# Moving the ranks and scatters of a routed block earlier in a fused attention and mixture-of-experts kernel

## The chip, the cores and the metric

The kernel runs on one core of a Trainium2 chip, in one launch. The metric is the device time of an execution in microseconds (us). "Before" is the kernel without the change; its times and one profiled execution are all that the prediction had.

## What is computed

```python
# r, k, v: (4, 8, 768, 48); w, u: (8, 48)
for t in range(S):
    cur = einsum('bhd,bhe->bhde', u * k[t], v[t])
    y[t] = einsum('bhd,bhde->bhe', r[t], state + cur)
    state = w * state + einsum('bhd,bhe->bhde', k[t], v[t])
x = y as (3072 tokens, 384)
x = relu(x @ w_in) ** 2 @ w_out                      # hidden size 2048
logits = x @ w_gate + log1p(exp(x @ w_noise)) * noise # 8 experts
top 2 experts of each token, softmax weights over the two
out = sum over the two: weight * relu(x @ w1[e]) @ w2[e]   # hidden size 1024
```

## The kernel before

The sequence is worked in chunks of 128 tokens (number q, 24 of them) and blocks of 512 (number j, 0 to 5). A block is four chunks.

Three stages overlap. A fixed list (`HEAD`) makes the first chunks' attention. Then a loop over the six blocks (L1063) runs the dense layer: for each f of 16, `mm1(j, f)` (L532, nine products of 128x128 by 128x512), its squared relu `gsplit` (L542, ScalarE and VectorE), and, two f later (`LAG = 2`), `mm2` (L558, mostly nine products again). After every such group stands one of 32 numbered places, 0 to 31, of the block: place 2f follows `mm1(j, f)`, place 2f+1 the `mm2` after it. All other work of the loop is put into these places by a hand-written table; the fraction of a number orders the work within a place. What is put there in block j: attention of the chunks of block j+1 (`CHUNKS`), the routing of block j-1 (`ROUTE`), and, in block 1, the clearing of the buffer `sent`. The third stage, after the loop, runs the experts and is not touched.

Each engine works through its own instructions in the order in which they were put. The places therefore order VectorE, GpSimd (POOL in the rows) and the DMA queue of SyncE as well as TensorE, but an engine runs ahead of the places as far as its inputs are ready.

Attention of a chunk in blocks 1 to 4, in the order of its steps: `pre` (L386; two GpSimd multiplies into `rk`), `p_tr r` and `p_tr k` (L426; a VectorE transpose, then a GpSimd multiply into `rT` or `kT`; the k one also issues the loads of the next chunk), `pre2` (L410; a VectorE sum `dg`, then GpSimd `am` and `vx`), `p_kv` (L494; 32 short products, VectorE adds into `Z`, two GpSimd multiplies of `Z`, L511), `p_a` (L454; 16 short products that read `kT` and `rT`, L459, then VectorE copies into `am`), `p_y` in two parts (L468; 24 short products with `Z`, then 32 with `am`, all L477), and `p_x` (L515). In block 1 the chunks are 8 to 11.

Routing of a block: four times `r_row` (logits), `r_soft1` to `r_sel` (small VectorE work), `r_w1` (one ScalarE exponential), `r_rank` (L701; three small products and seven VectorE operations: the place `si` of every token in `sent`), `r_w2` (L685; eight VectorE operations: weights into `row`), and eight times `r_send` (L729): a small GpSimd memset and one indirect DMA from GpSimd (L732) that scatters 128 rows of 393 floats to `sent`.

`zeros(e)` (L366) clears the places of expert e in `sent`, 1,375.5 KB each, from SyncE; the eight of them are put into block 1, places 3.6 to 13.6. Every scatter writes somewhere in `sent`, so the first one waits for all eight clearings; only the scatters among themselves are declared independent (L735). `zero_out` (L375) clears the output in five parts of 960 KB from SyncE, and its first call fills a zero tile that takes over the memory of the one `zeros` reads.

Of the kernel before, what the change touches and what calls it, by code (L numbers as in the profile page):

```python
# [64 lines left out]
         (3.13, 4.58, 7.33, 8.47),  # L65
         (3.22, 3.43, 3.45, 4.38))

ROUTE = ((4.54, 6.46, 8.84, 9.01, 9.55, 9.63, 10.54, 11.58, 13.491, 14.56, 14.65, 21.81, 20.25,
# [5 lines left out]
CLEAR = {3: (8.7, 14.7, 26.7), 4: (8.7, 14.7)}  # L74
FETCH_00 = 16.7
TURN_00 = ((21.8, 22.8), (23.8, 24.8), (25.8, 26.8))

# [15 lines left out]
def body(ctx, tc, r, k, v, w, u, w_in, w_out, w_gate, w_noise, noise, w1, w2, out):  # L93
# [969 lines left out]
    for j in range(NB):  # L1063
        slots = [[] for _ in range(2 * NF)]

        def put(n, fn, *args):
            k = int(n)
            slots[k].append((n - k, len(slots[k]), lambda: fn(*args)))
# [15 lines left out]
        if j == 1:  # L1084
            for i, n in enumerate(SPLIT_AT):
                put(n, split_out, i)
            for e in range(E):
                put(e * 3 // 2 + 3.6, zeros, e)
        for i, n in enumerate(CLEAR.get(j, ())):
            put(n, zero_out, i + sum(len(c) for k, c in CLEAR.items() if k < j), sum(map(len, CLEAR.values())))  # L1090
        if j:
            plan = [(r_row, i) for i in range(TPB)] + [(fn,) for fn in (r_soft1, r_soft2, r_soft3, r_top1, r_top2, r_sel, r_w1, r_rank, r_w2)]
            plan += [(r_send, *divmod(i, 2)) for i in range(2 * TPB)]
            for n, (fn, *args) in zip(ROUTE[0 if j == 1 else 1 if j < NB - 1 else 2], plan):
                put(n, fn, j - 1, *args)
# [171 lines left out]
```

## Time and profile before

| what | us |
|---|---|
| median of 3 runs | 951.79 (951.4 to 951.82) |
| the profiled execution, its own time | 954.92 |
| span of the profiled execution, first to last instruction | 953.1 |
| TensorE (PE) busy in it | 938.8 |
| GpSimd (POOL) busy in it | 349.2 |

The profiled execution took 3.1 us more than the median, and 1.8 us of its time lie around its span. Block 1 begins 118.5 us after the span's start, block 2 at 204.2, block 3 at 287.5, block 4 at 371.6, block 5 at 455.2.

### The profile page before, as it was taken

How to read it: one execution, taken by the hardware profiler on the slowest of the kernel's cores; microseconds unless marked ns; L12 is line 12 of the kernel's file. 1: busy time of each engine (PE TensorE's matmuls, PEld its weight loads, DVE VectorE, ACT ScalarE, POOL GpSimd, SP SyncE). 2: the span in 40 equal slices, each digit the busy share in tenths (PEclk: the TensorE clock that was granted, in tenths of full speed). 3: DMA queues.
4: the chain of work that ended last, by engine and by line, in shares of the span. 5: the costliest groups of instructions: out<-in, count | busy, mean ns of one | idle time of the engine just before them, and what ended most of it. 6: DMA issues, size and time to landing. Idle time of an engine off the chain costs nothing.

```text
span 953.1 us, 17746 instructions
## 1 busy us (share of the span) xinstructions
PE 938.8 (98%) x6845; PEld 805.3 (84%) x6845; DVE 540.4 (57%) x982; ACT 432.9 (45%) x792; POOL 349.2 (37%) x406
## 2 busy tenths in 40 slices
PE   8899999999999999999999999999999999999997
PEld 7677787778778878877888899999999898989987
DVE  8999756636845663684254564554545555356420
ACT  5666655334434444443555542443444444444321
POOL 6665353544573354455030344122121221212112
PEclk9999999999999999999999999999999999999999
DMA  7655379932432464442024367466545565545212
GB/s 179 165 163 165 96 191 302 244 108 64 94 104 56 111 153 122 111 99 86 1 100 93 108 134 188 104 135 135 130 97 115 120 121 109 114 92 109 36 21 37
DMA packets 193233, 112.32 MB, mean 118 GB/s; under 512 B 131777, under 2 KB 185698, under 8 KB 193122
## 3 DMA queue, kind: packets, MB, share of 16 engines
q1 hardware_dynamic: 181698, 91.03, 37.7%
q0 software_dynamic: 10624, 19.74, 11.3%
q8 instruction: 75, 1.23, 0.5%
q14 instruction: 36, 0.29, 0.1%
q10 hardware_dynamic: 800, 0.02, 0.0%
HBM read 74.64 MB, written 36.12 MB: 116 GB/s over the span
## 4 chain that ended last, share of the span: by engine, by line
PE 90%; DVE 5%; issue 1%; POOL 1%; ACT 1%; DMA 1%; POOLq 0%; DVEq 0%; ACTq 0%
PE ph L540 20%; PE xo L571 19%; PE ph L861 19%; PE y L918 14%; PE y L949 4%; PE att L477 3%; PE ph L949 2%; PE att L459 2%; PE att L604 2%; PE y L861 2%; PE xo L565 1%; PE att L962 1%; PE att L503 1%; DVE am L463 1%; DVE t L279 1%
## 5 line engine op out<-in xcount | busy, mean ns | idle before, releaser
L929 POOL DMA_INDIRECT out<-yt,id x56 | 87.1, 1556 | 298.1 <-ACT yt L927 257.4
L555 DVE TENSOR_TENSOR gl<-g,gh 128x512 fp32r<-128x512 f32 x90 | 77.2, 857 | 127.3 <-ACT gh L553 124.2
L904 DVE SCALAR_TENSOR_TENSOR hl<-ph,hh 128x512 fp32r<-128x512 f32 (+1 forms) x112 | 66.9, 599 | 113.1 <-ACT hh L903 109.2
L545 ACT ACTIVATE rt<-ph 128x512 f32<-128x512 f32 x96 | 57.1, 595 | 150.9 <-PE ph L540 146.4
L540 PE MATMUL ph<-x1h,wih 128*128 128x512 f32 x288 | 119.4, 414 | 0.0
L861 PE MATMUL ph<-xh,w0h 128*128 128x512 f32 (+3 forms) x336 | 118.1, 352 | 0.0
L861 PE MATMUL ph<-xl,w0h 128*128 128x512 f32 (+3 forms) x336 | 116.3, 346 | 0.2 <-DVE xl L830 0.2
L861 PE MATMUL ph<-xh,w0l 128*128 128x512 f32 (+3 forms) x336 | 116.1, 346 | 0.0
L540 PE MATMUL ph<-x1h,wil 128*128 128x512 f32 x288 | 112.4, 390 | 0.0
L540 PE MATMUL ph<-x1l,wih 128*128 128x512 f32 x288 | 112.3, 391 | 0.0
L571 PE MATMUL xo<-gh,wol 128*128 128x512 f32 x270 | 105.9, 392 | 0.0
L903 ACT ACTIVATE hh<-ph 128x512 fp32r<-128x512 f32 (+1 forms) x112 | 58.6, 524 | 88.9 <-PE ph L861 84.0
L918 PE MATMUL y<-w1h,hh 128*128 128x384 f32 x256 | 85.7, 335 | 0.0
L918 PE MATMUL y<-w1l,hh 128*128 128x384 f32 x256 | 85.6, 335 | 0.0
L918 PE MATMUL y<-w1h,hl 128*128 128x384 f32 x256 | 85.6, 334 | 0.0
L732 POOL DMA_INDIRECT sent<-row,si x48 | 50.3, 1049 | 61.4 <-DVE gl L555 45.0
L571 PE MATMUL xo<-gh,woh 128*128 128x512 f32 x180 | 71.6, 398 | 0.0
L571 PE MATMUL xo<-gl,woh 128*128 128x512 f32 x180 | 70.1, 390 | 0.0
L861 PEld LDWEIGHTS ph<-xl,w0h 128*128 128x128 f32 x336 | 63.3, 188 | 8.0 <-DVE xl L830 1.3
L861 PEld LDWEIGHTS ph<-xh,w0l 128*128 128x128 f32 x336 | 63.2, 188 | 7.7
L861 PEld LDWEIGHTS ph<-xh,w0h 128*128 128x128 f32 x336 | 63.3, 188 | 6.9 <-ACT xh L829 0.3
L540 PEld LDWEIGHTS ph<-x1h,wih 128*128 128x128 f32 x288 | 54.0, 188 | 16.4 <-issue 3.7
(234 smaller groups left out, 2145.5 us busy)
## 6 DMA issues: line engine op xcount, KB each, us to landing
ws<-in_moe_w SPq DMA_DIRECT2D x128, 96.0 KB
ws<-in_moe_w SPq DMA_DIRECT2D x32, 384.0 KB
sent<-zero SPq DMA_DIRECT2D x8, 1375.5 KB
G<-sent SPq DMA_DIRECT2D x36, 192.0 KB
stg<-in_moe_w_in SPq DMA_DIRECT2D x8, 768.0 KB
stg<-in_moe_w_out SPq DMA_DIRECT2D x8, 768.0 KB
out<-zero SPq DMA_DIRECT2D x5, 960.0 KB
lv<-in_v SPq DMA_DIRECT2D x24, 192.0 KB
```

The source lines that it names most:

```text
L477: nc.tensor.matmul(pb[32 * n:32 * n + 32, d, :], x, y, skip_group_check=True, **kw)
L540: nc.tensor.matmul(ph, wt[qi][:, d, sl], xt[j][:, d, :], start=(n == 0), stop=(n == 3 * KD - 1))
L545: nc.scalar.activation(rt, ph, AF.Relu)
L555: nc.vector.tensor_tensor(gl, g, gh.bitcast(F32), op=OP.subtract)
L571: nc.tensor.matmul(XO[j][:, d, :], wt[qi][:, fo, sl], gt, start=(f == 0 and n == 0), stop=(f == NF - 1 and n == 2))
L732: st = nc.gpsimd.indirect_dma_start(out=sent, in_=s["row"][:, i, :], in_offset=None, out_offset=bass.IndirectOffsetOnAxis(ap=s["si"][:, i, ...
L861: nc.tensor.matmul(ph[:, c], wt[:, d, sl], xt[:, d, c], start=(m == 0), stop=(m == 3 * KD - 1))
L903: nc.scalar.activation(hh[:, :n], ph, AF.Relu)
L904: nc.vector.scalar_tensor_tensor(hl[:, :n], ph, 0.0, hh[:, :n].bitcast(F32), op0=OP.max, op1=OP.subtract)
L918: nc.tensor.matmul(py, ht[:, sl], wt[:, fo, :], start=(m == 0), stop=(m == 3 * NF2 - 1))
L929: st = nc.gpsimd.indirect_dma_start(out=out, in_=yt, in_offset=None, compute_op=OP.add, out_offset=bass.IndirectOffsetOnAxis(ap=IDX[e, un] ...
L949: nc.tensor.matmul(py[d][:, c], wt[:, fo, sl], ht[:, c], start=(m == 0), stop=(m == 3 * NF2 - 1))
```

## The change

It moves routing steps between places, and one of the five parts of the output clearing from block 3 to block 2. Nothing is added or removed.

```diff
-ROUTE = ((4.54, 6.46, 8.84, 9.01, 9.55, 9.63, 10.54, 11.58, 13.491, 14.56, 14.65, 21.81, 20.25,
-          25.32, 26.97, 30.88, 25.84, 25.99, 21.93, 31.39, 31.66),
-         (4.94, 7.82, 9.35, 9.61, 10.1, 13.34, 13.45, 13.47, 13.721, 14.31, 20.46, 19.12, 21.54,
-          24.75, 22.9, 28.29, 28.16, 23.33, 24.72, 21.55, 28.65),
+ROUTE = ((4.54, 6.46, 8.84, 9.01, 9.55, 9.63, 10.54, 11.58, 13.491, 14.56, 14.65, 16.9, 16.5,
+          18.4, 19.3, 20.2, 23.2, 24.0, 24.8, 25.6, 27.8),
+         (4.94, 7.82, 9.35, 9.61, 10.1, 13.34, 13.45, 13.47, 13.721, 14.31, 14.7, 16.1, 16.5,
+          17.6, 18.3, 19.6, 20.3, 21.8, 22.5, 27.4, 28.1),
          (4.22, 4.4, 5.4, 5.47, 5.64, 6.68, 7.8, 7.81, 8.7, 9.5, 9.6, 11.9, 11.6,
           12.6, 13.2, 13.8, 14.4, 15, 15.6, 16.2, 16.6))
-CLEAR = {3: (8.7, 14.7, 26.7), 4: (8.7, 14.7)}
+CLEAR = {2: (16.7,), 3: (8.7, 14.7), 4: (8.7, 14.7)}
```

The first row of `ROUTE` is for block 1, the second for blocks 2 to 4, the third for block 5. The last eleven numbers of a row are `r_w1`, `r_rank`, `r_w2` and the eight scatters. In block 1 the rank goes from place 21 to 16 and the scatters from places 21 to 31 to places 18 to 27; in blocks 2 to 4 the rank goes from 19 to 16, `r_w2` from 21 to 16, and the scatters from 21 to 28 to 17 to 22, with two at 27 and 28. The attention steps stay where they were: in block 1 `p_y` 0 of chunk 9 at 18.64, `pre2` of chunk 10 at 20.4, `p_kv` of chunk 9 at 21.33, `p_tr k` of chunk 10 at 22.28, `pre`, `p_tr r` of chunk 11 and `p_kv` of chunk 10 at 22.4, 22.61 and 22.63, `p_tr k` of chunk 11 at 24.26, `pre2` of chunk 11 at 25.89, `p_a` of chunk 11 at 28.47.

## Rows read from the trace of the kernel before

**Rows 1.** The page: busy us of each engine.
```profile
PE 938.8 (98%) x6845; PEld 805.3 (84%) x6845; DVE 540.4 (57%) x982; ACT 432.9 (45%) x792; POOL 349.2 (37%) x406
```

**Rows 2.** Waits of PE from 118 to 530 us: total, times, longest.
```profile
PE att L503 <- issue: 0.8, 2, 0.4
PE att L477 <- issue: 0.7, 2, 0.4
```

**Rows 3.** Chain that ended last, block 1: start, us, what.
```profile
162.00 2.04 PE xo L571 x9
...
185.75 0.79 PE att L477 x24
...
192.18 1.09 PE att L459 x16
193.27 2.27 PE xo L571 x9
...
198.81 1.01 PE att L477 x20
...
202.13 2.27 PE xo L571 x9
```

**Rows 4.** Timeline of PE, blocks 2 and 3: start, us, what.
```profile
265.62 0.55 PE L503 MATMUL att<-lv,kp 128*32 128x48 f32 x32
...
354.07 0.35 PE L503 MATMUL att<-lv,kp 128*32 128x48 f32 x15
...
355.84 0.50 PE L540 MATMUL ph<-x1h,wih 128*128 128x512 f32 x1
```

**Rows 5.** Timeline of SP: the last three clearings of `sent`.
```profile
158.85 6.72 SPq L372 DMA_DIRECT2D sent<-zero  x3
```

**Rows 6.** Stretches: us, busy of PE, PEld, DVE, ACT, POOL, clock, DMA share, GB/s.
```profile
174.00:176.00 2.00, 2.00 (x13) 1.37 (x16) 1.87 (x10) 0.00 (x0) 0.37 (x1) 1.00 1.08 297
176.00:178.00 2.00, 2.00 (x68) 1.84 (x68) 1.86 (x6) 1.75 (x3) 2.00 (x3) 1.00 1.15 188
```

**Rows 7.** The scatter's line, all of it: semaphore events of its queue.
```profile
L732 POOLq EVENT_SEMAPHORE  x11: 17/17/916, 177.8 to 560.8; - x11
```

**Rows 8.** Timeline of POOL, block 1: start, us, what [idle before].
```profile
175.63 1.90 POOL L421 TENSOR_TENSOR am<-ident,dg 128x1024 f32<-128x1024 f32 x1 [8.07 <-DVE dg L414]
...
177.72 1.08 POOL L511 TENSOR_TENSOR Z<-Z,wmid 48x192 f32<-48x192 f32 x2
...
179.85 1.20 POOL L732 DMA_INDIRECT sent<-row,si  x1 [0.91 <-POOL gap L731]
...
182.37 1.02 POOL L395 TENSOR_TENSOR rk<-lr,lk 128x384 f32<-128x384 f32 x1
...
184.44 1.74 POOL L432 TENSOR_TENSOR rT<-rT,pow 112x512 f32<-112x512 f32 x1
186.15 1.08 POOL L511 TENSOR_TENSOR Z<-Z,wmid 48x192 f32<-48x192 f32 x2
187.31 1.29 POOL L432 TENSOR_TENSOR kT<-kT,pow 112x512 f32<-112x512 f32 x1
188.54 0.09 POOL L731 MEMSET gap<- 1x1 f32 x1
...
191.31 1.90 POOL L421 TENSOR_TENSOR am<-ident,dg 128x1024 f32<-128x1024 f32 x1
```

**Rows 9.** Waits of POOL from 118 to 530 us: total, times, longest.
```profile
POOL Z L511 <- DMA sent<-row,si: 5.3, 3, 4.1
```

**Rows 10.** Timeline of DVE, blocks 1 and 2: start, us, what.
```profile
162.23 0.16 DVE L673 TENSOR_TENSOR tot<-pre,sel 128x8 bf16<-128x8 bf16 x1
...
257.79 0.18 DVE L711 TENSOR_TENSOR rk<-att,base 128x32 f32<-128x32 f32 x1
...
259.68 0.17 DVE L724 CAST si<-slot 128x8 int32<-128x8 f32 x1 [0.21 <-DVE slot L722]
```

**Rows 11.** The last stretch of the execution: columns of rows 6.
```profile
948.00:953.00 5.00, 0.00 (x0) 0.00 (x0) 0.00 (x0) 0.00 (x0) 0.89 (x1) 0.54 0.36 44
```

## Prediction

> **What bounds the kernel now.** I read the page's busy times first: TensorE works 938.8 of 953.1 us [rows 1], so time can be gained or lost only where TensorE waits, and a transfer or another engine matters only by making it wait. Next the waits of TensorE, in the loop alone: two pairs, 1.5 us in all, both named "issue", so no engine or transfer is seen to release them [rows 2]. Then the places. At the end of block 1 stand 56 short products in one row, and they take 202.13 - 198.81 = 3.32 us [rows 3]. Undisturbed, 24 take 0.79 [rows 3], so 56 some 1.84: 1.5 us are lost. In block 3 a `p_kv` of 32 products takes 355.84 - 354.07 = 1.77 us where one in block 2 takes 0.55 [rows 4]: 1.2 lost. So all that the touched loop can give back is 2.7 us, 0.28% of the median. Both gaps lie where scatters run beside long rows of short products.
>
> Everything else in the loop is a cost if it makes TensorE wait. So I followed, for each moved step, what stands behind it on its engine and when TensorE wants that.
>
> **Block 1: the scatters meet the clearing.** The first scatter waits for all eight clearings of `sent`. The last three were issued from 158.85 to 165.6 us [rows 5], and the DMA engines, with a share of 1.08, still moved 297 GB/s from 174 to 176 and fell to 188 only in the next 2 us [rows 6]. The scatter's queue passed its first semaphore event at 177.8 [rows 7], just before the scatter could have run anyway (179.85, [rows 8]). I take 177.8 as the landing; nothing ahead of it changes, so the change can't bring it forward.
>
> Now the order on GpSimd. Before, the first scatter (place 21.93) comes behind `am` and `vx` of chunk 10 and `Z` of chunk 9. After, three scatters (18.4, 19.3, 20.2) stand ahead of these. GpSimd reaches them in the 8.07 us that it now sits idle before 175.63 [rows 8], and blocks until 177.8. Queued behind the blocked scatter is everything GpSimd owes to attention. Step by step, with starts and distances of [rows 8]:
>
> - The first scatter starts up to 0.91 us after the step before it (the idle time at 179.85); I take 0.7 from the release, so 178.5, and 1.20 for itself. Two more take 191.31 - 188.54 = 2.77 with their memsets: 182.5.
> - `am` and `vx` 177.72 - 175.63 = 2.09: 184.6. `Z` of chunk 9 187.31 - 186.15 = 1.16: 185.7.
> - A multiply of `Z` behind scatters was seen to wait for their landing, three times, 4.1 us at most [rows 9]. Here 0 to 0.5, the third scatter having been issued 3 us earlier.
> - `kT` of chunk 10 188.54 - 187.31 = 1.23, the two `rk` 184.44 - 182.37 = 2.07, `rT` of chunk 11 1.3 (as `kT`) to 1.71, `Z` of chunk 10 1.16: together 5.8 to 6.2, so 191.5 to 192.4.
> - The scatters at 23.2 and 24.0, both ahead of `kT` of chunk 11 (24.26): 2.77. Then `kT` 1.23: it is ready at 195.5 to 196.4, where before it was ready at 188.5.
>
> TensorE wants that `kT` for `p_a` of chunk 11 at 192.18 [rows 3]. It waits 3.3 to 4.2 us. I take 3.4, near the lower figure, because some of the rows ran slowed beside other work, and 2.8 as the lower end. Earlier waits are inside this number, since its end is fixed by the clearing: `p_y` 0 of chunk 10 wants `Z` of chunk 9 at 185.75 [rows 3], which is now ready at 185.7 to 186.2, and the rank's products come at place 16, just before the group at 162.00 [rows 3], when `tot` is ready only at 162.23 + 0.16 = 162.39 [rows 10]: at most 0.5 each. What is late next is `am` of chunk 11, two scatters and itself behind `kT` (2.77 + about 1.9), at about 200.4, and VectorE's copies follow; TensorE, itself 3.4 late, wants them after 203 (198.81 + 3.4 + 0.79, [rows 3]) and finds them ready.
>
> **Blocks 2 to 4.** The rank costs VectorE 259.85 - 257.79 = 2.1 us [rows 10], and `r_w2`'s eight small operations I take at about 1.5 by the same row's pace (0.18 each). 3.6 us more at place 16 delays the `gl` that follow. They are wanted two f later, which is four large groups of 2.04 to 2.27 us [rows 3], over 8 us, so TensorE sees nothing. No clearing of `sent` is outstanding. On GpSimd six scatters of 1.4 us (half of 2.77, [rows 8]) fit into places 17 to 22, which hold few other GpSimd steps; nothing of chunk work behind them is wanted before place 24. Price 0; were the cover gone, 1.4 us a scatter.
>
> **The gaps.** In block 3 no scatter stands in places 23 to 26 any more. If its gap needs scatters beside the short products, 1.2 us come back. In block 1 the late start pushes the last scatters (24.8, 25.6, 27.8) to 196 to 202, so with the products 3.4 us later they meet the same row of 56 again; I expect 0 to 1.5 back. Whether the gaps exist in a run without the profiler is open too: the profiled execution took 3.1 us more than the median, enough to hold all of them. The bounds are 0 and 2.7; I take 0.6, half of block 3's.
>
> [...]
>
> **The output clearing.** A part of 960 KB occupies the DMA engines 3 to 5 us (at the 297 to 188 GB/s of [rows 6]). In block 2, place 16.7, it is queued on SyncE behind the loads of place 15.7 that VectorE wants at 17.96, and the next loads are wanted after place 22: hidden. If it did delay a wanted load, VectorE would be up to 5 us late, inside the 8 us of cover just named. In block 3 its absence shortens the 4.1 us that a `Z` multiply waited [rows 9], which TensorE never saw [rows 2]. 0.
>
> **Sum.** 3.4 - 0.6 = +2.8 us. Against the profiled execution's own 954.92 that is 957.7; against the median, 951.8 + 2.8 = 954.6.
>
> **Rivals.** I call a change of more than 0.2% (1.9 us) one that a measurement of this kernel can tell.
>
> - *Forecast, 44%:* GpSimd blocks behind the clearing and `p_a` of chunk 11 waits 2.8 to 4.1; 0 to 1.2 of the gaps return. 953.4 to 955.9.
> - *Wait and both gaps cured, 18%:* 3.4 - 2.7 = +0.7, 952.5. For it: places 24 and 26 are free of scatters by design; against: block 1's late scatters.
> - *Faster, 17%:* the blocked scatters cost TensorE nothing, because the clearing lands before about 174.4, 3.4 us sooner, which is where the sum for `kT` meets 192.18; both gaps go. 951.8 - 2.7 = 949.1, or 949.6 with the rank's wait. Against: the DMA rate to 176 [rows 6].
> - *Nothing moves, 13%:* the wait is hidden and the gaps are the recorder's: 951.8.
> - *The clock falls, 8%:* TensorE's clock was granted at 1.00 (2.4 GHz) through all its short waits and fell to 0.54 in the last stretch, where it had nothing to do [rows 11]. If a wait of 3.4 us dropped it to 1.2 GHz, each large group of nine would take 2.04 us more [rows 3] until it rose; one or two: 957 to 959. [...]
>
> The likeliest gives 954.6, by itself 953.4 to 955.9. The range goes down to the faster case and leaves out the clock: 949.1 to 956.2. Slower 44 + 8 = 52%; within 0.2% 18 + 13 = 31%; faster 17%.
>
> **What would show it.** In the profile after: GpSimd idle from about 168 to 178 before a scatter in block 1; `p_a` of chunk 11 (L459) waiting for GpSimd about 3 us near 192 to 196; block 2 beginning 2 to 3.5 us later than 204.2; no gap in `p_kv` of block 3. The prediction is wrong if the first scatter of block 1 runs well before 177, or if `kT` of chunk 11 is ready by 192.

## The result, and the profile after

The changed kernel took 959.01 us (median of 4 runs, 958.37 to 961.0) against 951.79 for the kernel before (4 runs, 951.4 to 951.82): a ratio of 1.008, 95% interval 1.0064 to 1.0096. That is 7.2 us slower where +2.8 (954.6) was forecast, and outside the predicted range of 949.1 to 956.2. The profiled execution took 961.0 with a span of 959.2.

The blocks, each from its first `mm1` product (L540) to the next block's, in the two profiles:

| block | before, us | after, us |
|---|---|---|
| 1 | 85.76 (with the 1.5 us gap) | 92.73 |
| 2 | 83.23 | 83.88 |
| 3 | 84.09 (with the 1.2 us gap) | 82.77 |
| 4 | 83.65 | 83.81 |

So the loss is in block 1; block 2's 0.65 holds a stop of 0.4 us in a row of short products at 281.9. The waits of TensorE in the loop after (total, times, longest); none of them stood in [rows 2]:

```profile
PE att L459 <- POOL gap L731: 3.8, 1, 3.8
PE att L477 <- POOL Z L511: 0.2, 1, 0.2
PE att L707 <- DVE pre L671: 0.2, 1, 0.2
```

The first is `p_a` of chunk 11, the place that the prediction named. (The releaser is printed as the memset behind `kT` on GpSimd, because `kT` ended just before it.) GpSimd's timeline of block 1 after, to be laid beside [rows 8]:

```profile
167.73 0.09 POOL L731 MEMSET gap<- 1x1 f32 x1
179.05 1.56 POOL L732 DMA_INDIRECT sent<-row,si  x1 [11.23 <-ACT gh L553]
...
182.21 0.97 POOL L732 DMA_INDIRECT sent<-row,si  x1 [0.22 <-issue]
183.21 1.91 POOL L421 TENSOR_TENSOR am<-ident,dg 128x1024 f32<-128x1024 f32 x1
...
186.67 0.51 POOL L511 TENSOR_TENSOR Z<-Z,wmid 48x192 f32<-48x192 f32 x1 [0.87 <-DMA sent<-row,si]
187.26 1.28 POOL L432 TENSOR_TENSOR kT<-kT,pow 112x512 f32<-112x512 f32 x1
188.49 1.48 POOL L395 TENSOR_TENSOR rk<-lr,lk 128x384 f32<-128x384 f32 x1
...
191.00 1.27 POOL L432 TENSOR_TENSOR rT<-rT,pow 112x512 f32<-112x512 f32 x1
192.24 1.53 POOL L511 TENSOR_TENSOR Z<-Z,wmid 48x192 f32<-48x192 f32 x2
...
196.43 1.50 POOL L432 TENSOR_TENSOR kT<-kT,pow 112x512 f32<-112x512 f32 x1
```

GpSimd stands for 11.23 us before the first scatter, all its attention work behind it. The releaser printed there, a ScalarE step, writes nothing that a scatter reads. The scatter's queue stood at one of its semaphores for 8.98 us (8984 ns, the longest event of its line), from 169.1 to 178.1, when the indices `si` had been ready since 169.8:

```profile
L732 POOLq EVENT_SEMAPHORE  x13: 17/17/8984, 166.7 to 567.5; - x13
```

What landed at 178.0 was the last clearing; its semaphore is the one that ended that event. The traffic runs down there (columns as in [rows 6]):

```profile
174.00:176.00 2.00, 2.00 (x39) 1.59 (x39) 1.77 (x4) 0.04 (x1) 0.00 (x0) 1.00 1.06 300
176.00:178.00 2.00, 2.00 (x61) 1.57 (x63) 0.00 (x0) 0.94 (x2) 0.00 (x0) 1.00 1.16 209
196.00:198.00 2.00, 0.01 (x2) 0.02 (x2) 0.69 (x1) 0.09 (x1) 1.90 (x3) 0.93 0.61 214
198.00:200.00 2.00, 2.00 (x17) 1.78 (x17) 0.00 (x0) 0.00 (x0) 1.67 (x3) 0.50 0.21 74
...
206.00:208.00 2.00, 2.00 (x24) 1.43 (x26) 0.55 (x1) 0.25 (x1) 0.00 (x0) 1.00 0.49 98
```

The column after POOL is TensorE's granted clock. From 196 to 198 TensorE did nothing; then, from 197.73 on and for 6.83 us, the clock was 0.50 while TensorE was fully busy, and 1.00 again by 206. The chain that ended last after, to be laid beside [rows 3]:

```profile
196.43 1.50 POOL kT L432
...
197.99 2.08 PE att L459 x16
200.06 4.14 PE xo L571 x9
204.20 1.19 PE att L477 x32
205.39 2.27 PE ph L540 x9
207.65 1.67 PE att L477 x56
```

`p_a` takes 2.08 in place of 1.09, the nine products of `mm2` 4.14 in place of 2.27. And the row of 56 takes 1.67, not 3.32: its gap is gone. So is block 3's (start, us, what):

```profile
356.31 0.48 PE att L503 x32
```

Two amounts make up the 8.6 us of block 1 above an undisturbed block of 84.11 (the profile of the second experiment):

- **Late.** Counted from the block's start, `p_a` of chunk 11 begins at 197.99 - 118.70 = 79.3; before it was 192.18 - 118.48 = 73.7 [rows 3]. That is 5.6 us: the 3.8 of the wait, 0.65 around the rank's three products at place 16, and 1.1 in `p_y` 0 and `p_a` of chunk 10, which took longer behind the late `Z` and `kT`.
- **Half clock.** From the start of `p_a` to the next `mm1` it is 205.39 - 197.99 = 7.4 us, where before it was (198.81 - 2.27) - 192.18 = 4.4. That is 3.0.

### The profile page after: what moved, and what is told of

Its sections match the earlier page's. It is cut to its first block, busy times and chain, and to the rows that moved or that the text cites. A ratio compares the mean times of both kernels' runs of the same rounds, so it can differ in the third digit from the quotient of the medians.

```text
span 959.2 us, 17751 instructions
## 1 busy us (share of the span) xinstructions
PE 942.2 (98%) x6845; PEld 807.7 (84%) x6845; DVE 541.5 (56%) x982; ACT 433.4 (45%) x792; POOL 349.7 (36%) x406
## 3 DMA queue, kind: packets, MB, share of 16 engines
q8 instruction: 75, 1.23, 0.5%
## 4 chain that ended last, share of the span: by engine, by line
PE 83%; DVE 7%; POOL 3%; DMA 3%; issue 2%; ACT 1%; SPq 1%; POOLq 0%; DVEq 0%; ACTq 0%
PE ph L861 19%; PE ph L540 16%; PE xo L571 16%; PE y L918 13%; PE y L949 5%; PE att L477 2%; PE ph L949 2%; PE att L604 2%; PE y L861 2%; PE att L459 2%; DMA sent<-row,si 1%; PE xo L565 1%; DVE am L463 1%; PE att L962 1%; DVE gl L555 1%
## 5 line engine op out<-in xcount | busy, mean ns | idle before, releaser
L555 DVE TENSOR_TENSOR gl<-g,gh 128x512 fp32r<-128x512 f32 x90 | 83.2, 924 | 139.2 <-ACT gh L553 139.1
L540 PE MATMUL ph<-x1h,wih 128*128 128x512 f32 x288 | 119.2, 414 | 0.0
L540 PE MATMUL ph<-x1h,wil 128*128 128x512 f32 x288 | 112.5, 391 | 0.0
L540 PE MATMUL ph<-x1l,wih 128*128 128x512 f32 x288 | 112.3, 391 | 0.0
L918 PE MATMUL y<-w1h,hh 128*128 128x384 f32 x256 | 85.7, 335 | 0.0
L540 PEld LDWEIGHTS ph<-x1h,wih 128*128 128x128 f32 x288 | 54.0, 188 | 16.4 <-issue 3.5
```

The lines of the kernel that those rows point to most:

```text
L540: nc.tensor.matmul(ph, wt[qi][:, d, sl], xt[j][:, d, :], start=(n == 0), stop=(n == 3 * KD - 1))
L555: nc.vector.tensor_tensor(gl, g, gh.bitcast(F32), op=OP.subtract)
L918: nc.tensor.matmul(py, ht[:, sl], wt[:, fo, :], start=(m == 0), stop=(m == 3 * NF2 - 1))
```

## The experiments

The theory: block 1's scatters alone make the loss, first through `kT` of chunk 11, then through the clock that falls in the wait. The main rival: the wait is small change, and the loss is spread over the new row of blocks 2 to 4 and the moved clearing; later, that the half clock costs nothing that the wait had not cost already.

Three chips were used. On the first (four kernels) the kernel before took 951.78 us (19 runs), on the second 955.08 (23 runs), on the third 954.92 (17 runs), so each result is set against its own. The record names no chip for the result above and for the first profile of the kernel before; by its times the result belongs with the first chip.

**Block 1's row alone.** The new first row of `ROUTE`; all else as before.

```diff
-ROUTE = ((4.54, ..., 14.65, 21.81, 20.25, 25.32, 26.97, 30.88, 25.84, 25.99, 21.93, 31.39, 31.66),
+ROUTE = ((4.54, ..., 14.65, 16.9, 16.5, 18.4, 19.3, 20.2, 23.2, 24.0, 24.8, 25.6, 27.8),
```

> Only block 1's row of ROUTE is the changed one; blocks 2 to 4 and the output clearing are as before. Clearing theory (three scatters ahead of GpSimd's attention steps wait for the clearings of sent, kT of chunk 11 is late, TensorE waits 3.8 us and its clock then halves): the whole loss and no return from block 3, so 6 to 9 us over before, 958 to 961, with a TensorE wait of 3.5 to 4.2 us at the p_a of chunk 11 and a stretch at half clock behind it. Spread theory (the loss comes from ranks and weights that now crowd VectorE in blocks 1 to 4, or from the moved output clearing): at most a third of the loss, 952 to 954.5.

Measured: 959.97 (959.81 to 960.07), ratio 1.0087 [1.0072, 1.0103], +8.2. The same wait of 3.8 at L459, the clock at 0.5 for 6.83 us behind it, block 1 92.13. Block 1's row alone makes a loss as large as the whole one. In this execution block 3, scheduled as before, took 82.77: its gap did not occur.

**Blocks 2 to 4 and the clearing alone.** The second row of `ROUTE` and `CLEAR` of the change; block 1 as before.

> The other part alone: blocks 2 to 4 and the output clearing as changed, block 1 as before. Clearing theory: no loss; if the gap of 1.2 us in block 3's p_kv is there without the profiler too and goes, 950.3 to 951.2, and if the gap is only the profiler's, 951.5 to 952.2. Spread theory: 4 to 6 us over before, 956 to 958.

Measured: 953.39 (951.77 to 953.91, 11 runs), ratio 1.0015 [1.0006, 1.0024], +1.6. The profiled execution took 951.77, and no wait of TensorE stands in its loop. The median lies above both ranges of the first expectation and well below that of the second: the loss is not spread, but a remainder of 0.6 to 2.3 us, by the interval, is there that was not expected, and the last two runs below take it up. The two parts alone make 8.2 + 1.6 = 9.8 us and the change 7.2, so they do not simply add up. Block 1, scheduled as before, took 84.11: no gap there either.

**Two scatters behind `kT`.** The change, with the scatters of places 23.2 and 24.0 put behind `kT` of chunk 11 (24.26).

```diff
-          18.4, 19.3, 20.2, 23.2, 24.0, 24.8, 25.6, 27.8),
+          18.4, 19.3, 20.2, 24.3, 24.4, 24.8, 25.6, 27.8),
```

> The changed kernel, but the two scatters of places 23.2 and 24.0 in block 1 stand at 24.3 and 24.4, just behind kT of chunk 11. Clearing theory: kT of chunk 11 is ready about 2.7 us sooner, TensorE waits about 1 us at the p_a of chunk 11, and, the wait being short, the clock stays at 2.4 GHz: 951 to 953.5. If the clock fell for another reason than the length of this wait: 955 to 957. Spread theory: unchanged, 958 to 960.

Measured: 956.19 (956.04 to 957.43), ratio 1.0047 [1.0031, 1.0062], +4.4. The waits of TensorE in the loop:

```profile
PE att L477 <- DVE am L463: 1.1, 1, 1.1
PE att L459 <- POOL gap L731: 1.0, 1, 1.0
...
```

Taking 2.6 us from the chain ahead of `kT` takes 2.8 from the wait at L459. The clock stays at 1.00 in block 1. But `am` of chunk 11 is now behind the moved scatters, and TensorE waits 1.1 us for it: block 1 takes 87.72, and the time is 2.7 above the expected range. (The profiled execution, 957.43, is 1.2 over the median. Its clock fell for 6.83 us in block 0, whose schedule is the same in every kernel here, and block 0 took 86.97 where it takes 85.7 without a fall.)

**All eight scatters behind `kT`.** As before it, but the eight at 24.3, 24.4, 24.8, 25.6, 26.0, 26.1, 26.2 and 27.8.

> The changed kernel, but all eight scatters of block 1 stand behind kT of chunk 11 (24.3, 24.4, 24.8, 25.6, 26.0, 26.1, 26.2, 27.8); the rank stays early. Clearing theory: no wait of TensorE at the p_a of chunk 11, no fall of the clock, 949.5 to 952, the spread being what the gaps of blocks 1 and 3 give back. Spread theory: still 956 or more, since the ranks stay early.

Measured: 953.68 (953.21 to 955.61, 9 runs), ratio 1.0022 [1.0012, 1.0032], +1.9. One wait in the loop is left:

```profile
PE att L707 <- DVE pre L671: 0.2, 1, 0.2
```

`am` of chunk 10 starts 56.6 us into the block (57.2 before the change, [rows 8]), and block 1 takes 84.76, 0.65 above the undisturbed 84.11; the rank's products at place 16 are what is left of the change there. The time is 1.7 above the expected range; what block 1 does not explain of the +1.9, some 1.2, is near the remainder of blocks 2 to 4 and the clearing alone (+1.6). With the scatters behind `kT` the wait at L459 is gone, so the order on GpSimd made it.

**Work in the wait.** The change, with 30 dummy transposes just ahead of `p_a` of chunk 11.

```diff
     def p_a(q, *tag):
-        a = A[q]
+        a = A[q]; [nc.tensor.transpose(pw[:, :P], ident, ident) for pw in ([bank()] if q == 11 else []) for _ in range(30)]
```

> The changed kernel with 30 dummy transposes of 128x128 on TensorE just ahead of p_a of chunk 11 (work that is not in the computation and goes into a bank of its own). They fill the 3.8 us in which TensorE waited for kT of chunk 11. Clock theory (3.4 us of the loss are the 6.83 us at a granted clock of 0.5 that follow the idle wait): GpSimd's chain is as late as in the changed kernel, so p_a still starts near 198, but the clock is then 1.00, the groups after it take 2.27 again and block 1 is 3 to 3.5 shorter: 955.3 to 956.5. Rival (the half clock has another cause than the idle wait, or the groups would be that long anyway): 958.4 to 960, with the clock at 0.5 in the profile all the same.

Measured on the second chip: 958.87 (956.71 to 959.69), ratio 1.0033 [1.0022, 1.0044] to a kernel before of 955.08, +3.8, above the range that was put in microseconds of the first chip. The clock did not fall in block 1, which took 88.81 (it did fall in block 0, for 3.41 us). As the chip was another one, the run was made again beside the changed kernel itself, on the third chip:

> The changed kernel once more, on the same chip as the kernel with 30 filler transposes and the kernel before. In the executions with the two 1.5-us gaps the kernel before took 955.1, in those without 951.8, and the changed kernel has no long row beside its scatters in either place. If the gaps are what tells the two apart, the changed kernel is 958.4 to 960 whichever of the two the kernel before shows (its 3.8 of wait and 3.4 of half clock stay), so +7.2 against a kernel before of 951.8, and +3.5 to +5 against one of 955.1.

> The changed kernel with 30 dummy transposes ahead of p_a of chunk 11, as in the run filler, now beside the changed kernel itself. Clock theory: 2.5 to 4 us faster than the changed kernel of the same runs, with no half clock behind p_a of chunk 11. Rival (the half clock costs nothing that the wait had not cost already): within 1 us of it.

Measured: the changed kernel 960.64 (959.12 to 961.27), ratio 1.0059 [1.0045, 1.0072]; with the dummy work 957.55 (956.69 to 959.07), ratio 1.0032 [1.002, 1.0043]: 3.1 us faster for work added. The first, +5.7, came out 0.6 above what was expected of it. The stretch of `p_a` in the changed kernel's profile:

```profile
196.00:198.00 2.00, 0.16 (x2) 0.17 (x4) 0.66 (x1) 0.00 (x0) 1.78 (x4) 1.00 0.55 200
198.00:200.00 2.00, 2.00 (x17) 1.78 (x18) 0.00 (x0) 0.00 (x0) 1.78 (x3) 0.51 0.26 92
```

and with the dummy work:

```profile
196.00:198.00 2.00, 1.49 (x19) 1.19 (x18) 0.00 (x0) 0.00 (x0) 1.76 (x4) 1.00 0.11 35
198.00:200.00 2.00, 2.00 (x9) 1.40 (x8) 0.00 (x0) 0.00 (x0) 1.84 (x2) 1.00 0.45 171
```

TensorE's timeline with the dummy work (L455) shows that the wait is covered, not removed; 0.51 us of it stay idle:

```profile
192.75 3.44 PE L455 MATMUL att<-ident 128*128 128x128 f32 x30
196.69 1.16 PE L459 MATMUL att<-rT,kT 48*128 48x128 f32 x16 [0.51 <-POOL gap L731]
```

From the start of `p_a` to the next `mm1` it is 201.06 - 196.69 = 4.4 us here, as in the kernel before, and 203.84 - 197.84 = 6.0 in the changed kernel's profile of this chip, where the half clock lasted 3.41 us, not 6.83. So the profiles put 1.6 of the 3.1 down to the clock; `p_a` also began 0.6 sooner in the block, and block 2 was 0.4 shorter. The rival is out, and the clock cost 1.6 us in the one profile and 3.0 in the other.

**Half as much of it.** 12 transposes in place of 30.

> As filler, but with 12 transposes, some 1.6 us by the pace of the warm-up transposes (0.13 each), so that about 2.2 of the 3.8 us stay idle. If an idle stretch of 2.2 us is enough for the clock to fall, 958.4 to 960 and 0.5 in the profile for some 6.8 us; if it is not, 955.3 to 956.5 as with filler. The trace of the kernel before had no idle stretch of that length, so I hold both possible and lean to no fall.

Measured on the second chip: 960.51 (959.73 to 963.94), ratio 1.0061 [1.0045, 1.0077], +5.4 and 1.6 more than with 30. I had leaned to no fall; the clock fell, for 3.41 us from 198.34 on, 1.6 us after an idle stretch of 2.47 had ended:

```profile
192.77 1.47 PE L455 MATMUL att<-ident 128*128 128x128 f32 x12
196.71 1.16 PE L459 MATMUL att<-rT,kT 48*128 48x128 f32 x16 [2.47 <-POOL gap L731]
```

**The clearings sooner.** The change, with the eight clearings of `sent` at places 2.6 to 9.6.

```diff
-put(e * 3 // 2 + 3.6, zeros, e)
+put(e + 2.6, zeros, e)
```

> The changed kernel, but the eight clearings of sent are put into places 2.6 to 9.6 in place of 3.6 to 13.6. The places of the scatters are those of the change. Theory (the late landing of the clearings blocks GpSimd, and kT with it): the first scatter can start before 179, some 3 to 8 us sooner as far as the DMA engines, full from 132 to 178, allow; three scatters are over by about 176, kT of chunk 11 is ready by 192 to 194, TensorE waits at most 2 us and keeps its clock: 951.5 to 955. Rival (GpSimd is late through the scatters' own time, not through the clearing): the wait stays near 3.8 and the time 958 to 960. Second rival: the loads of chunk 10 and 11, now behind the clearings on SyncE's queue, come late, and TensorE waits for these instead: over 955 with a wait at another line.

Measured on the second chip: 958.08 (956.07 to 961.2, 11 runs), ratio 1.0029 [1.002, 1.0039], +3.0. GpSimd's timeline:

```profile
175.31 0.09 POOL L731 MEMSET gap<- 1x1 f32 x1
178.35 1.20 POOL L732 DMA_INDIRECT sent<-row,si  x1 [2.95 <-DVE gl L555]
...
194.00 1.27 POOL L432 TENSOR_TENSOR kT<-kT,pow 112x512 f32<-112x512 f32 x1
```

The scatter did not start sooner to speak of. The loads of the next chunk now stand behind the clearings, and VectorE stood 7.03 us for them. So GpSimd came to the scatter at 175.4 and not at 167.8, and `si`, which the scatter reads, was written only by 177.4 (169.8 in the changed kernel):

```profile
170.22 1.10 DVE L430 STREAM_TRANSPOSE rT<-rp 128x512 f32<-128x512 f32 x1 [7.03 <-DMA rp<-in_r]
...
177.24 0.17 DVE L724 CAST si<-slot 128x8 int32<-128x8 f32 x1
```

The last clearing had landed by 176.3, so here the scatter waited for `si`, and the run does not test what an earlier landing alone would have given. From the first scatter to `kT` of chunk 11 the same steps ran shorter (194.00 - 178.35 = 15.7 us, where the changed kernel has 196.43 - 179.05 = 17.4); `kT` was ready 76.1 us into the block and not 79.2, and the wait at L459 is gone. But TensorE itself came to that `p_a` only 81.4 us into the block (73.7 in the kernel before). It had lost time elsewhere, in a `p_kv` whose 32 products meet the three scatters of 178.35 to 182.1. The chain there:

```profile
180.00 0.45 issue
180.45 0.32 PE att L503 x4
180.77 0.45 issue
181.22 0.26 PE att L503 x2
181.48 0.48 issue
181.96 0.24 PE att L503 x2
182.20 0.51 issue
182.72 0.26 PE att L503
182.97 4.14 PE xo L571 x9
```

Four stops of half a microsecond, 1.9 us in all; at 182.19, with three of them past, the clock fell for 6.83 us, and the nine products that follow take 4.14. This is the slowest of the eleven executions, with a mean granted clock of 0.993; eight of the others show 0.998 or 0.999, too much for a fall of that length (6.83 us at half clock take 0.0036 off the mean). So the chain shows what can happen here, not what the median's +3.0 is made of. The second rival had the late loads right; the theory is not decided by this run, which does not give the price of the wait by itself.

**The clearing of the output alone.** `CLEAR = {2: (16.7,), 3: (8.7, 14.7), 4: (8.7, 14.7)}`, all else as before.

> The kernel before with the one part of the output clearing moved from block 3, place 26.7, to block 2, place 16.7, and nothing else. The rows of blocks 2 to 4 together with this move gave +1.5 us in the median with no wait of TensorE in the profile. If the clearing is what costs, +1 to +2: 952.8 to 953.8. If it is free, as the prediction had it: 951.2 to 952.4, and the 1.5 belong to the steps of blocks 2 to 4.

Measured on the second chip: 955.62 (954.16 to 956.94, 11 runs), ratio 1.0002 [0.9993, 1.0011]. Free, as predicted.

**Blocks 2 to 4's row alone, and the kernel before beside it.**

> The kernel before with the row of ROUTE for blocks 2 to 4 alone; block 1 and the output clearing stay as they were. Moving the clearing alone gave nothing (ratio 1.0002). So the +1.5 us that the row and the clearing gave together should be the row's: +1 to +2 against a kernel before without gaps; against one with both gaps, block 3's gap is cured, so -0.5 to +0.7. If the row is free, as the prediction had it, 0 in the first case and -1.2 to -1.7 in the second.

> The kernel before, for a profile of this chip. Either block 1 takes 85.8 and block 3 84.1 to 84.4 (both gaps there) and the time is 954.5 to 955.5, or 84.1 and 82.8 (no gaps) and it is 951.4 to 952.4. A profile with gaps and a time near 952, or one without and a time near 955, would say that the gaps come with the recording and cost a run without it nothing.

Measured on the third chip: the row alone 954.11 (11 runs), ratio 0.9993 [0.9984, 1.0002], -0.8 and so between the two expectations; the kernel before 954.62 in its profiled execution, beside a median of 954.92. The chain of the kernel before, block 1:

```profile
199.17 0.85 PE att L477 x19
200.02 0.31 issue
200.33 0.27 PE att L477
200.60 0.43 issue
201.03 1.30 PE att L477 x30
```

Both gaps are there (block 1 85.61, block 3 83.96), as they are on the second chip in the kernel with the clearing alone (85.79 and 84.43); on the first chip two profiles could have shown one each, and neither did (block 3 82.77 with block 1's row alone, block 1 84.11 with the rows of blocks 2 to 4). Together they are 2.7 to 3.4 us, and the kernel before is 3.1 to 3.3 slower on the second and third chips than on the first. The sizes agree, so the gaps are the likely difference between the chips, in the timed runs too; that is argued from a few profiles. Whether the recording has a part in them stays open, as every timed run here has a recorded span and clock. The row for blocks 2 to 4 takes block 3's gap away where there is one (83.15) and has a small price of its own: block 4 takes 83.80 in the profile of the row alone, and 83.65 with the old row. In blocks 2 and 4 the rank's products used to stand next to `p_y`'s short products; at place 16 they stand alone, and the large group behind them takes 2.16 us up to the next group's first product, where one behind a large group takes 2.04. That accounts for 0.1 to 0.2 a block, not for all of the +1.6 on the first chip.

## Why the prediction was wrong

**What bounds the kernel, and where to look: right.** The change worked through GpSimd's order in block 1, on `kT` of chunk 11, at L459, and blocks 2 to 4 hid nearly all of theirs (+1.6 together with the clearing on the first chip, -0.8 alone on the third).

**The wait: right in mechanism, too small in size.** "It waits 3.3 to 4.2 us. I take 3.4, near the lower figure" is the first term that failed: the lateness was 5.6 in the changed kernel's profile and 5.4 in the other. The release at about 178 was right (the last clearing landed at 178.0), with some luck in the reading: in the kernel before GpSimd came to the scatter's semaphores only behind `Z` at 177.72 [rows 8], so the event at 177.8 marks its arrival as much as the landing, which was at 177.9. What failed is the sum behind it. The first scatter started at 179.05, not 178.5, and took 1.56, not 1.20; `Z` of chunk 9 waited 0.87 for the landing of the scatters, not 0 to 0.5; the two `rk` took 2.5, not 2.07; `Z` of chunk 10 1.58, not 1.16; the last `kT` 1.50, not 1.23. Each is a little over the row that was taken for it, and all stand in one line, so `kT` was ready at 197.93, not 195.5 to 196.4. The lower figure was taken because "some of the rows ran slowed beside other work"; the chain after ran beside the same work. Only 3.8 of it shows as one wait, since earlier waits took their part of the lateness, as predicted.

**The clock: named, and left out of the sum.** "The clock falls, 8%" was the case that came about. That its 957 to 959 misses the median by only 0.01 us is luck in part: the wait in it was too small and the gaps were taken off. The evidence given against it, a clock of 1.00 through all the short waits [rows 11], was of waits of 0.4 in the stretch that was read. The kernel before has a longer one in block 0, 1.4 us at L459 in its first profile, without a fall there; in its profile on the third chip that wait is 1.75 and the clock falls 1.7 us after its end:

```profile
40.00:42.00 2.00, 1.36 (x15) 1.26 (x16) 1.92 (x3) 2.00 (x7) 2.00 (x2) 1.00 0.86 298
42.00:44.00 2.00, 2.00 (x7) 1.53 (x6) 1.91 (x3) 1.97 (x6) 1.93 (x3) 0.59 0.23 93
```

The length of that wait alone does not tell which way it goes. In the fourteen profiles it is 0.9 to 1.75 us, and the clock falls by its end or within 2 us after it in five (waits of 1.0, 1.2, 1.7, 1.75 and 1.75), not in the other nine, the changed kernel's two profiles (1.75 and 1.74) among them. All four profiles with the longer waits at `p_a` of chunk 11 (three of 3.8, one of 2.47) have a fall there. By these runs a fall was the likelier case for a wait of 3.4, not one in twelve; one trace before the change could not show it. Its price was put at one or two groups of 2.04 us, 2 to 4; measured it is 3.0 (6.83 us at half clock) and 1.6 (3.41 us), so the price was fair and what failed is the 0 in the sum. No run shows the 2.4 and 1.2 GHz of the recorded texts: the traces give the clock as a share alone, 1.00 before each fall and 0.50 in it. Nor do the runs show one length of wait that parts a fall from none: behind one of 1.0 us it fell, behind one of 1.75 it did not.

**The gaps: 0.6 was taken back, and there was nothing to take.** The profiled execution of before had both gaps and the runs behind its median of 951.79 most likely did not, by the comparison of the chips above. So "against the median" the term is 0. Both gaps did go in the changed kernel, block 1's as well, which I had put at 0 to 1.5.

**The output clearing: 0 predicted, 0 measured** (1.0002). **The rank's wait:** "at most 0.5" was 0.65 with its seam, part of the lateness of `p_a`.

Put together for the profile of the third chip: 5.4 late and 1.6 of half clock are 7.0, and the block is 91.12 - 84.11 = 7.0 longer. That agrees with the 7.2 of the result. In the first profile it is 5.6 + 3.0 = 8.6; that execution took 961.0 at a mean granted clock of 0.994, the result's other three 958.4 to 959.1 at 0.997, so they stood less long at half clock. By the third chip's profile, what the forecast of 2.8 missed of the 7.2 is 5.4 - 3.4 = 2.0 of lateness, 1.6 of clock and 0.6 of gaps: 4.2 of 4.4.

What stays open: why 11 runs with blocks 2 to 4 and the clearing alone spread from 951.8 to 953.9 on the first chip where the profile shows no wait; and what makes the gaps. They stand beside scatters in rows of short products, but not beside every scatter. No version here beats both kernels by more than a run can tell: the row of blocks 2 to 4 alone came nearest, at 0.9993 on one chip.

## What to carry to other kernels

When a step is put earlier on an in-order engine, ask what it still waits for; if that is a transfer, everything behind it waits for the transfer as well (here GpSimd stood 11.23 us ahead of the first scatter, until 179.05, and the last `kT` was ready at 197.93 where before it was ready at 188.5), and each of those steps is to be priced at its slower rows, since they add up in one line. A wait on TensorE can have a second price, the groups that follow it at half clock: behind the waits of 3.8 and 2.47 us the clock stood at 0.50 for 6.83 or 3.41 us here, at a price of 3.0 and 1.6 us in the two profiles of the changed kernel. Where a wait of a few microseconds can't be avoided, work that fills nearly all of it can be worth more than it costs (here 30 dummy transposes, 3.44 us, won 3.1 us of the changed kernel, and 12, 1.47 us, did not keep the clock up). And a gap seen in one profiled execution is not yet a gap in the timed runs (here that execution took 954.92, with both gaps, against a median of 951.79): compare that execution's own time with the median before counting on its return.

## What the runs showed of the hardware that had not been expected

- The clock's fall inside the work lasted 6.83 us in some executions and 3.41 in others, of the same kernel too, and nothing between was seen.
- It fell with every idle stretch of 3.8 or 2.47 us, with five of fourteen of 0.9 to 1.75 us in block 0 (one of 1.0 among the five, two of 1.75 among the nine without), and after three stops of 0.45 to 0.48 us that began 0.7 to 0.8 us apart.
- The kernel before differs by 3.3 us between chips, which is about the size of its two gaps; the gaps were in profiles from two chips, and on the chip with the shorter time the two profiles that could show one had none.
